# Hand-written engine orders made anew in a fused attention and state-space kernel

## The chip, the cores and the metric

The kernel runs on one core of a Trainium2 chip. The core has TensorE (PE in the profile, its weight loads PEld), VectorE (DVE), ScalarE (ACT), GpSimd (POOL) and SyncE (SP), each with an instruction stream of its own that it works through in order, and 16 DMA engines behind several queues. The metric is the device time of one execution in microseconds (us); lower is better.

## The reference

Two independent computations on sequences of 2048 positions and 640 channels; their outputs are put side by side into a bf16 array of 1 x 2048 x 1280.

```python
# part A: attention, 32 heads of 20, each position sees itself and 7 positions 2, 4 .. 14 back
qkv    = x @ wqkv                                # 2048x640 @ 640x1920
logits = (q . k at the 8 positions) * 20**-0.5   # masked where the position is < 0
a      = (softmax(logits) weighted sum of v) @ wo
# part B: a state-space layer, 192 complex states for each channel
dt = exp(log_dt)
K[d, l] = Re( sum_n C[d,n] * exp(dt*A[d,n]*l) * dt*B[d,n] )      # 640 x 2048, from 640 x 192 parameters
y = irfft(rfft(u, 4096) * rfft(K, 4096))[:2048] + u * Dskip      # causal convolution of u with K
out = concat([a, y], axis=-1)
```

## The kernel before

Part B's kernel K is not made by 2048 exponentials for each state. A position l is split as l = x + 8b with 20 values of x and 33 of b, and exp(dt·A·l) becomes a product of two tables. The 640 channels are cut into five groups (c = 0 to 4) of 128. For each group, `Xtab` (20 complex rows of 192 states) and `Ytab` (33 rows) are built on DVE from a few starting powers; then `kgen_part` on TensorE multiplies them, channel by channel. These are the stages that the orders below name:

- **Prologue.** `prep` brings in the parameters and transposes them on TensorE; ACT and DVE make phases and magnitudes. `am0`, `gens0`, `genm0` make the starting powers of group 0 (ACT exponentials, ACT sines, DVE products), `am1`, `gens1`, `genm1` those of groups 1 to 4, which SP stores to DRAM (`Gdram`). `weights` forms C·dt·B on DVE and has SP store it. `load` brings in the transposes of x (20 in all, 5 for each quarter of the sequence) and constants.
- **Projections** `k0 q0 v0 … v3`: three for each quarter of the sequence, each 25 matmuls of 128 x 512 (L515), five ACT copies (L516) into the tile `st`, of which there are two, and one SP store (L519 for v) to DRAM (`qkd`, `vd`).
- **Tables** of group c: `tab` (SP loads `Xg` from `Gdram`, one tile) and `taby` (five SP loads into `Ytab`, one tile, L330), `mag` (16 ACT exponentials, L345), `xtab` (32 DVE instructions, L306 and L307; `Xtab` has two tiles), `ypos` (12 on DVE, two on POOL), `yneg` (four on DVE, L351 two of them). `yneg` takes mag's two halves.
- **Table products** `kgen{c}0` to `kgen{c}3`: one opening product of zeros and 128 small ones (L398, L403) for each, then one ACT copy (L405) into `Kd`, of which there are two; PSUM tag "b", four buffers.
- **Convolution.** `u` turns u around through DRAM (`Udram`) on POOL and DVE. For each group: `u{c}` (SP loads `U`, 16 matmuls, 8 ACT copies), `spread{c}` (36 matmuls and 16, 12 copies), `spec`/`spec{c}` (128 matmuls L452, 16 copies L456: the spectra of u of group 0, and of K of group c with u of the next), `swap{c}` (SP), `prod{c}` (four DVE products), `inv{c}` (64 matmuls L479, 8 copies into Z; Z of groups 0 to 2 goes to DRAM). The last step, `last00` to `last07` and `last10` to `last13`, turns blocks of positions back with the table `HB` (four POOL loads, `hb`), adds u·Dskip (`uD`; `ud`, `ud0` to `ud4`) and stores.
- **Attention** for each quarter b: `fetch{b}` and `fetchv{b}` (SP loads `qk` and `vb` from DRAM), `logits{b}` (ten DVE products L562, 44 matmuls L566, three ACT functions, one DVE product into `attn`), `av{b}` (ten DVE products L592, 160 matmuls L598, six copies into `oT`), `out{b}` (40 matmuls L611, eight copies, four stores L614). The products of L562 and L592 share three buffers; L566's sums and L598's sums have two PSUM buffers each.

The tables' memory is released after `kgen4`; `HB`, `uD` and the Z of groups 3 and 4 lie in it. The projections' memory is released after the last projection and holds `U`, the constant `T` (cT, `load2`) and others after that.

What sets the order is the dictionary `SEQ`: for each engine a list of words, written out by hand. A word `kgen00:129` means the next 129 instructions that stage kgen00 has on this engine; a word without a number means one. The function `chain` walks the list and ties each instruction to the one before it. So each engine issues exactly in this order, SP's list being the order in which SP issues its DMAs; semaphores add what one engine waits for from another. With `at(name)` the code says which stage the instructions inside it belong to. The instructions of `magnitudes`, `gens` and the first `ymag` also go through `pin`, which ties ACT's functions to one another in the order in which the code makes them.

Of the kernel before, what the change touches and what calls it, by code (L numbers as in the profile page):

```python
# [13 lines left out]
bf16 = mybir.dt.bfloat16  # L14
# [113 lines left out]
def att_consts_np():  # L128
# [11 lines left out]
prep:30 weights:15 k0:2 weights:15 k0:2 weights:15 k0:5 weights:15 k0:16 q0:25 v0:25 k1:25 q1:25 v1:25 k2:25 q2:16 kgen00:129 q2:9 kgen01 kgen02  # L140
kgen03:129 kgen02:128 kgen01:128 v2:25 k3:10 logits0:4 k3:2 logits0:4 k3:6 logits0:4 k3:7 q3:10 logits0:8 q3:15 logits0:4 v3:10 kgen10:33 kgen11:33
kgen12 kgen13:129 logits0:4 kgen10:64 logits0:8 v3:4 logits0:4 v3:6 kgen10:32 v3:5 logits0:4 kgen11:96 kgen12:96 av0:32 kgen12:32 av0:48 u0:8 av0:5
u0:2 av0:8 u0:2 av0:9 u0:2 av0:9 u0:2 av0:17 spec:20 av0 spec:12 av0:31 spec:32 out0:4 spec out0:3 spec:31 logits1:4 out0:2 spec out0 spec:16 out0:2
spec:15 out0:3 logits1:2 u1:8 logits1:2 out0:2 u1:2 out0:2 u1:2 out0 u1:2 logits1:4 u1:2 out0:2 spread0:8 out0:2 spread0:8 logits1:2 spread0:20
logits1:2 out0 logits1:4 spread0:8 logits1:4 out0:2 spread0:4 out0:2 spread0:2 out0 spread0:2 logits1:4 spec0:32 logits1:4 spec0 out0:4 spec0:16
out0:3 spec0:16 out0:2 spec0:15 out0 spec0:48 inv0:57 kgen20:129 inv0:7 logits1:8 kgen21 kgen22 kgen23:33 u2:2 logits1:2 kgen23:32 u2:2 logits1:2
kgen23:64 u2:2 kgen22:32 u2:2 kgen22:32 u2:4 kgen22:64 u2:4 kgen21:128 spread1:36 av1:6 spread1:8 av1:5 spread1:2 av1:8 spread1:2 av1:9 spread1:2
av1:9 spread1:2 av1:27 spec1:49 av1:15 spec1:16 av1 spec1:63 inv1:64 kgen30 kgen31:33 kgen30:32 kgen31:96 kgen30:96 kgen32 kgen33 u3:2 kgen33:32 u3:2
kgen33:32 u3:2 kgen33:32 u3:4 kgen33:32 kgen32:32 u3:6 kgen32:32 spread2:16 kgen32:32 spread2:20 kgen32:32 av1:21 spread2:8 av1:5 spread2:2 av1:8
spread2:4 av1:2 spread2:2 av1:12 spec2:6 logits2:4 spec2:26 av1:8 spec2 av1:19 spec2:16 av1:5 logits2:4 spec2:31 out1:2 logits2:4 spec2 out1:2  # L150
spec2:16 out1 spec2:15 out1:2 spec2 out1:3 spec2:15 out1:20 inv2:32 out1:7 inv2:25 kgen40:33 inv2:5 logits2:4 inv2:2 out1:2 kgen40:96 logits2:4 out1
logits2:4 kgen41 kgen42 kgen43 u4:2 kgen43:64 u4:2 kgen43:32 u4:2 kgen43:32 logits2:6 u4:2 logits2:2 u4:2 logits2:4 kgen42:32 u4:4 logits2:4 kgen42:32
u4:2 spread3:8 logits2:2 kgen42:32 spread3:8 logits2:2 spread3:12 kgen42:32 spread3:8 kgen41:32 spread3:6 kgen41:32 spread3:2 kgen41:32 spread3:6
av2:15 spread3:2 av2:33 kgen41:32 spec3:32 av2:8 spec3 av2:8 spec3:95 av2:43 inv3:32 av2:21 inv3:25 spread4:16 inv3:4 spread4:12 inv3 spread4:8 inv3:2
av2:16 spread4:16 av2:16 spec4:32 logits3:4 out2:2 spec4 logits3:2 spec4:16 logits3:2 out2:2 spec4:16 logits3:4 spec4:15 out2 spec4 logits3:4 spec4:16
out2:2 spec4:15 logits3:4 spec4 out2:2 spec4:15 logits3:4 out2:20 inv4:32 out2 logits3:4 out2:5 inv4:25 last00:18 inv4:7 logits3:12 out2:5 last01
logits3:2 last01:8 logits3:2 last01 last02 last01:8 last02:17 last03 av3:32 last03:9 last04 last03:8 av3:17 last04:17 av3:37 last05 av3:39 last05:17
av3:35 last06:10 out3:10 last06:8 out3:10 last07 out3:10 last07:17 last10:34 last11:17 out3:10 last11:17 last12:34 last13:34
""",
    mybir.EngineType.Activation: """  # L160
prep:11 am0:2 prep am0:9 weights:2 gens0:13 weights gens0:4 weights gens0:4 k0 gens0 mag0:3 k0 mag0:3 k0 mag0:2 k0 mag0:3 k0 mag0:2 q0 mag0:3 am1:11
gens1:5 q0:3 gens1 q0 v0:3 gens1 v0:2 gens1:2 k1:2 gens1 k1 gens1 k1 gens1 k1 gens1 q1 gens1 q1 gens1 q1 gens1 q1 gens1 q1 v1 gens1:2 v1 gens1 v1
gens1 v1:2 k2:2 gens1:2 k2:2 mag1:5 k2 mag1:3 q2:2 mag1:8 q2 kgen00 q2:2 kgen03 kgen02 kgen01 v2:5 k3:5 q3:5 mag2:16 kgen13 v3:2 logits0:2 v3:2 kgen10
v3 logits0:2 kgen11 kgen12 av0:2 u0:8 av0:2 spec:4 av0:2 spec:4 out0 spec:4 out0 spec:4 out0 u1:7 spread0:4 u1 out0 spread0:8 out0:2 spec0:6 out0
spec0:10 mag3:14 inv0:4 mag3:2 inv0:3 out0 kgen20 inv0 logits1:2 u2:2 logits1:2 kgen23 u2:4 kgen22 u2:2 kgen21 spread1:12 av1:2 spec1:16 mag4:8 inv1:7
mag4 inv1 mag4:7 kgen31 kgen30 u3:5 kgen33 u3:3 spread2:4 kgen32 spread2:8 av1:2 spec2:6 av1 spec2:4 av1 spec2:4 out1 spec2:2 out1:5 inv2:4 out1
inv2:4 kgen40 out1 u4:3 kgen43 u4:4 logits2:2 u4 spread3:2 logits2 spread3 logits2 spread3 kgen42 spread3:8 kgen41 spec3:16 av2:2 inv3:4 av2:2 inv3:3
spread4:4 inv3 spread4:8 av2:2 spec4:10 out2 spec4:6 out2:3 inv4:2 out2 inv4:2 out2:2 inv4:3 last00:2 inv4 logits3:2 out2 last01 logits3:2 last01
last02:2 av3:2 last03:2 av3:2 last04:2 av3:2 out3 last05:2 out3:3 last06:2 last07:2 out3:4 last10:2 last11:2 last12:2 last13:2
""",  # L170
    mybir.EngineType.DVE: """
prep:11 gens0 prep gens0:2 prep:2 gens0:2 genm0 gens0:2 genm0 gens0:2 genm0 gens0:2 genm0 gens0:2 genm0 gens0:2 genm0 gens0:2 genm0 gens0:2 genm0
gens0:2 genm0 gens0 weights genm0 ypos0 genm0 weights:10 xtab0 weights xtab0 gens1 xtab0:2 gens1 xtab0:2 gens1 xtab0:2 gens1 xtab0:2 u xtab0:8 gens1
genm1 xtab0 genm1 xtab0 gens1 xtab0:2 genm1 xtab0:4 gens1 xtab0:4 gens1 xtab0:2 gens1 ypos0 genm1 gens1:2 ypos0 gens1 genm1 gens1 ypos0 gens1 genm1
gens1 ypos0 gens1 genm1 gens1 ypos0 genm1 gens1:2 ypos0 gens1 genm1 gens1 ypos0 genm1 yneg0 gens1 yneg0 ypos0:2 genm1 ypos0:2 u yneg0:2 xtab1:22 u
xtab1:4 logits0 xtab1:4 logits0 xtab1:2 logits0 ypos1:2 logits0 ypos1:2 logits0 ypos1:2 logits0 ypos1:4 yneg1 ypos1:2 yneg1:2 u xtab2:2 yneg1 xtab2:2
logits0 xtab2:2 logits0 xtab2:2 logits0 xtab2:2 logits0 xtab2:8 logits0 xtab2 av0:8 xtab2 av0:2 xtab2 ypos2 xtab2 logits1 xtab2:4 logits1 xtab2:4
logits1 xtab2:2 logits1 ypos2 logits1 ypos2:2 logits1 ypos2:2 logits1 ypos2:2 logits1 ypos2 xtab3 ypos2 yneg2 ypos2:2 yneg2 xtab3 yneg2 prod0 xtab3
prod0:2 xtab3 prod0 xtab3:2 yneg2 xtab3:2 logits1 xtab3:2 logits1 xtab3:10 logits1 xtab3:2 av1 xtab3:4 av1 xtab3:4 av1 xtab3:2 ypos3:4 av1 ypos3:2
xtab4 ypos3:2 av1 ypos3:2 yneg3 ypos3:2 yneg3 xtab4 prod1 xtab4 prod1:2 xtab4 prod1 xtab4:2 yneg3 xtab4:2 yneg3 xtab4:2 av1 xtab4:2 av1 xtab4:2 av1  # L180
xtab4:18 av1:2 ypos4:2 logits2 ypos4:4 logits2 ypos4:2 logits2 yneg4 ypos4 yneg4 ypos4 prod2 ypos4 prod2:2 ypos4 prod2 yneg4 logits2 yneg4 logits2:7
av2:7 prod3:3 av2 prod3 av2 ud1 ud4 ud0 ud2 ud3 av2 logits3:6 prod4:3 logits3 prod4 logits3:4 av3:10
""",
    mybir.EngineType.Pool: """
load ypos0 load:6 prep:18 load:7 ypos0 u:13 load2:4 u ypos1:2 kgen03:4 u:6 logits0:7 ypos2:2 kgen13:4 ypos3:2 kgen23:4 ypos4:2 kgen33:4 hb kgen43:4
hb:3
""",
    mybir.EngineType.SP: """
prep:12 load:15 weights k0 weights genm1:2 q0 genm1 v0 genm1:2 k1 genm1:3 q1 genm1:2 v1 genm1 k2 tab1 fetchv0:8 fetch0:2 q2 fetch0 taby1:5 v2 tab2
fetch0:2 k3 fetch1 q3 fetch1:2 v3 u0 load2 taby2:2 fetchv1:4 taby2:3 u1 fetchv1:4 out0 fetch1 swap0:2 tab3 u2 fetch1 out0 fetch2:2 out0:2 fetch2 swap1  # L190
inv0 swap1 u3 taby3:3 tab4 taby3:2 fetchv2:4 swap2:2 inv1 u4 taby4:5 fetchv2:4 fetch2 out1:3 fetch2 swap3:2 inv2 fetch3 out1 fetch3:2 last00:3
last01:3 fetchv3:4 ud swap4:2 fetchv3:4 fetch3:2 out2:3 last02:3 last00:4 out2 last03:3 last04:3 last01 last02:4 last01 last05:3 last06:3 last01:2
last03:4 last07:3 last04:4 last05:4 out3:2 last06:4 last07:2 out3 last07:2 out3 last10:4 last11:4 last12:4 last13:4
""",
}

def partB_prep(tc, pools, early, Gd):

    nc = tc.nc
    V = nc.vector
    pp, psp, ident = pools["prep"], pools["psum"], pools["ident"]
    Wd = NCH * CW
    nat, ldt = early
    hp = pp.tile([128, 1], f32, name="half_pi")
    nc.gpsimd.memset(hp[:], float(np.pi / 2))
    pools["half_pi"] = hp[:]
    dtb = pp.tile([128, NCH], bf16, name="dtb")
# [408 lines left out]
def kernel(  # L618
# [17 lines left out]
    nc = tc.nc  # L636
# [311 lines left out]
```

## Time and profile before

| | |
|---|---|
| runs, each the time of one execution | 412.6, 424.4, 828.71 us; median 424.4 |
| span of the profiled execution | 415.1 us |
| granted TensorE clock in it, mean | 0.889 of full speed |
| busy: PE, PEld, DVE, ACT, POOL | 316.8, 196.1, 307.1, 262.1, 50.4 us |
| DMA moved | 70.67 MB in 78841 packets, of them 35264 under 512 B |

The profiled execution's own time is its span, 415.1 us; it lies between the two lower runs. A stretch of the timeline shows, in this order: from and to, length, then for PE, PEld, DVE, ACT and POOL the busy time and the number of instructions, the granted clock, the busy share of the DMA engines, and GB/s. In a timeline each row is: when the instruction began, how long it took, its engine, its line, its operation, and its tiles; in brackets the idle time of that engine just before it and what ended that idle time ("issue": nothing that the profile shows). A row may stand for several alike (x13). In SyncE's queue (SPq) the rows are DMA issues.

### The profile page before, as it was taken

Reading aid. Unit: us, or ns where it says so; the run is one execution under the profiler, and the core shown is the slowest. Engines: PE = TensorE matmul, PEld = TensorE weight load, DVE = VectorE, ACT = ScalarE, POOL = GpSimd, SP = SyncE. Lnnn points to the kernel's source line nnn. Section 1 sums busy time; section 2 is a strip of 40 time slices with the busy share of each in tenths; the row PEclk is TensorE's granted clock in tenths of the full one; section 3 lists DMA queues with packets and bytes.
Section 4 is the critical chain, followed back from the end, with each engine's and each line's share of the span. In section 5 each row is a group of like instructions: output and inputs, shape, how many; then the busy total and the mean of one; then the engine's idle time right before and its main releaser. Section 6 shows DMA issues by size and latency. Waiting matters only on the chain. (4 is left out here: it accounts for less than half of the span.)

```text
span 415.1 us, 13105 instructions
## 1 busy us (share of the span) xinstructions
PE 316.8 (76%) x5645; PEld 196.1 (47%) x5654; DVE 307.1 (74%) x445; ACT 262.1 (63%) x570; POOL 50.4 (12%) x101
## 2 busy tenths in 40 slices
PE   0569249989359988799788886799999875897781
PEld 0224114335233355356476556565666663475561
DVE  0558978995974999589999599959972765786500
ACT  0587977987004533489976596469747977573552
POOL 7453300004014010200000200011000400000000
PEclk9999959999759999589979696779999988799996
DMA  5999765668998847869308530727166499616656
GB/s 75 217 212 178 202 164 190 214 216 260 207 213 205 271 126 171 233 146 254 114 17 230 154 86 2 205 64 154 51 195 209 138 369 313 137 49 177 160 134 95
DMA packets 78841, 70.67 MB, mean 170 GB/s; under 512 B 35264, under 2 KB 73904, under 8 KB 76992
## 3 DMA queue, kind: packets, MB, share of 16 engines
q1 hardware_dynamic: 71616, 54.96, 51.3%
q0 software_dynamic: 4144, 12.18, 11.9%
q10 hardware_dynamic: 3024, 2.70, 2.9%
q8 instruction: 44, 0.72, 0.7%
q14 instruction: 13, 0.11, 0.1%
HBM read 37.82 MB, written 23.65 MB: 148 GB/s over the span
## 5 line engine op out<-in xcount | busy, mean ns | idle before, releaser
L515 PE MATMUL ps_p<-xT,w 128*128 128x512 bf16 x291 | 76.4, 409 | 20.9 <-ACT st L516 15.4
L515 PEld LDWEIGHTS <-w 128*128 128x128 bf16 x300 | 30.0, 103 | 60.3 <-issue 33.3
L562 DVE TENSOR_TENSOR prod<-qk 128x2048 bf16<-128x2048 bf16 x40 | 48.2, 1225 | 11.6 <-PE ps_l L566 8.9
L592 DVE TENSOR_TENSOR p<-vb,attn 128x2048 bf16<-128x2048 bf16 x40 | 47.4, 1224 | 12.1 <-PE ps_o L598 12.0
L438 ACT CAST A<-ps_f 128x512 bf16<-128x512 f32 x80 | 42.8, 613 | 19.0 <-PE ps_f L437 18.6
L516 ACT CAST st<-ps_p 128x512 bf16<-128x512 f32 x60 | 34.6, 586 | 23.1 <-PE ps_p L515 21.1
L456 ACT CAST Sp<-ps_f 128x512 bf16<-128x512 f32 (+1 forms) x96 | 42.4, 564 | 4.6 <-PE ps_f L452 3.5
L398 PE MATMUL ps_k<-Ytab,Xtab 128*20 128x33 bf16 x1280 | 29.7, 248 | 15.1 <-issue 15.1
L598 PE MATMUL ps_o<-p,cHs 64*32 64x256 bf16 x640 | 27.7, 297 | 12.5 <-DVE p L592 7.7
L452 PE MATMUL ps_f<-A,cT 64*128 64x128 bf16 (+1 forms) x768 | 29.4, 211 | 5.4 <-ACT Sp L456 3.5
L398 PEld LDWEIGHTS <-Xtab 128*20 128x20 bf16 x1280 | 23.3, 128 | 21.6 <-issue 20.2
L405 ACT CAST Kd<-ps_k 128x264 bf16<-128x264 f32 x20 | 7.6, 380 | 40.7 <-PE ps_k L403 40.5
L479 PE MATMUL ps_ia<-cE,Sp 128*128 128x128 bf16 x160 | 25.5, 254 | 8.0 <-DVE Sp L467 7.8
L452 PEld LDWEIGHTS <-cT 64*128 64x128 bf16 x768 | 21.7, 96 | 18.4 <-issue 17.1
L403 PE MATMUL ps_k<-Ytab,Xtab 64*20 64x33 bf16 x1280 | 27.4, 244 | 3.5 <-issue 3.5
L611 PE MATMUL ps_op<-wo,oT 128*128 128x320 bf16 x160 | 29.0, 301 | 0.7 <-ACT ob L612 0.6
L480 ACT CAST Z<-ps_ia 128x512 bf16<-128x512 f32 x40 | 22.4, 604 | 10.7 <-PE ps_ia L479 8.3
L403 PEld LDWEIGHTS <-Xtab 64*20 64x20 bf16 x1280 | 22.4, 123 | 8.0 <-issue 6.7
L479 PE MATMUL ps_ia<-cE,UT 128*128 128x128 bf16 x160 | 25.4, 253 | 0.0
L306 DVE TENSOR_TENSOR Xtab<-Xtab,Xg 128x768 bf16<-128x768 bf16 (+2 forms) x35 | 24.5, 699 | 0.3
L307 DVE TENSOR_TENSOR krtmp<-Xtab,Xg 128x768 bf16<-128x768 bf16 (+2 forms) x35 | 24.4, 698 | 0.0
L345 ACT ACTIVATE mag<-ta 128x192 bf16<-128x192 f32 x80 | 22.6, 397 | 1.2 <-DVE Ytab L351 1.2
(109 smaller groups left out, 571.0 us busy)
## 6 DMA issues: line engine op xcount, KB each, us to landing
qk<-qkd SPq DMA_DIRECT2D x20, 263.0 KB, 5.3
qkd<-st SPq DMA_DIRECT2D x8, 640.0 KB, 5.3
UT<-Sp SPq DMA_DIRECT2D x10, 512.0 KB, 6.7
Gdram<-cs SPq DMA_DIRECT2D x11, 384.0 KB, 3.0
HB<-k_HB POOLq DMA_DIRECT2D x4, 1024.0 KB, 16.1
vb<-vd SPq DMA_DIRECT2D x16, 196.5 KB, 5.0
Xg<-Gdram SPq DMA_DIRECT2D x4, 768.0 KB, 7.7
Zdram<-Z SPq DMA_DIRECT2D x3, 1024.0 KB, 8.6
```

The lines of the kernel that those rows point to most:

```text
L398: MM(o, lhsT=X[:, :, part, col], rhs=Y[:, :, part, col], start=False, stop=False, tile_position=(0, 32 * g), skip_group_check=True)
L403: MM(o, lhsT=X[hb:hb + 64, :, part - 2, col], rhs=Y[hb:hb + 64, :, part - 2, col], start=False, stop=(part == 3), tile_position=(hb, 32 * ...
L438: nc.scalar.copy(out=A1[:].rearrange("p k r s t -> p (k r) s t")[:, :, sig, 8 * q:8 * q + 8], in_=ps[:])
L452: nc.tensor.matmul(ps[h][:, kk], lhsT=C["T"][hs, k, 64 * (1 - r):64 * (1 - r) + 128], rhs=A1[hs, k, r, s0:s1, :].rearrange("p s t -> p (s ...
L456: nc.scalar.copy(out=o, in_=ps[h][:].rearrange("p k (s t) -> p s t k", t=64))
L479: nc.tensor.matmul(ps[:, i], lhsT=X[:, h, 4 * t:4 * t + 4, :].rearrange("p g k -> p (g k)"), rhs=C["E"][:, n_, :], start=(i == 0 and n_ == ...
L515: nc.tensor.matmul(ps[:], lhsT=self.w[which][:, kt, 128 * ct:128 * ct + 128], rhs=self.xT[:, kt, 512 * sc:512 * sc + 512], start=(kt == 0) ...
L516: nc.scalar.copy(out=st[:, ct], in_=ps[:])
L562: V.tensor_tensor(out=pr[:], in0=self.qk[b][ct][:, 0, HALO:].unsqueeze(1).to_broadcast([128, 4, PB]), in1=windows(self.qk[b][ct][:, 1, 8 - ...
L592: V.tensor_tensor(out=p2[:], in0=windows(self.v[b][t][:, 2 * qp:2 * qp + 2, 0:PH], 2, 4), in1=at[:].unsqueeze(2).to_broadcast([128, 4, 2, ...
L598: nc.tensor.matmul(ps[half][32 * q:32 * q + 32, t % 2], lhsT=C["Hs"][r], rhs=p2[r, m, q2, :], start=(t % 2 == 0 and m == 0), stop=(m == 3) ...
L611: nc.tensor.matmul(ps[:], lhsT=oT[:, t, 128 * s:128 * s + 128], rhs=self.wo_sb[:, t, 320 * eh:320 * eh + 320], start=(t == 0), stop=(t == 4))
```

## The change

Every list of `SEQ` is written anew, with all the instructions of the old ones. Around it, five edits of the code:

```diff
@@ partB_prep
-    hp = pp.tile([128, 1], f32, name="half_pi")
-    nc.gpsimd.memset(hp[:], float(np.pi / 2))
-    pools["half_pi"] = hp[:]
@@ PartA.load_w
-        self.nc.scalar.dma_start(out=t[:], in_=self.wqkv.rearrange("(kt k) c -> k kt c", k=128)[:, :, D * i:D * i + D])
+        self.nc.sync.dma_start(out=t[:], in_=self.wqkv.rearrange("(kt k) c -> k kt c", k=128)[:, :, D * i:D * i + D])
@@ the order of the activation tables
-    tail = []
     def pin(ins):
-        if tail:
-            tc.add_manual_dep(ins.ins, tail[-1], mybir.DependencyInfo(mybir.DependencyClass.NoSync, mybir.DependencyReason.DATA), reason="order of the activation tables")
-        tail.append(ins.ins.name)
         return ins
@@ the prologue
-    with at("prep"):
+    with at("set"):
+        hp = pp.tile([128, 1], f32, name="half_pi")
+        nc.gpsimd.memset(hp[:], float(np.pi / 2))
+        pools["half_pi"] = hp[:]
+        zw = cst.tile([128, 128], bf16, name="zw")
+        nc.gpsimd.memset(zw[:], 0.0)
+        pools["zero"] = zw[:]
+    with at("params"):
...
-        for i in range(5):
-            a.load_x(i)
-        for nm in "kqv":
-            a.load_w(nm)
+    with at("params2"):
         for i, nm in enumerate(("B_C_re", "B_C_im", "B_B_re", "B_B_im")):
             par(nm, nat[2 + i], [nc.gpsimd])
-        zw = cst.tile([128, 128], bf16, name="zw")
-        nc.gpsimd.memset(zw[:], 0.0)
-        pools["zero"] = zw[:]
+    for nm in "kqv":
+        with at("w" + nm):
+            a.load_w(nm)
+    for sc in range(4):
+        with at(f"x{sc}"):
+            for i in range(5):
+                a.load_x(5 * sc + i)
+    with at("prep"):
         ta, wi, weights = partB_prep(tc, pools, (nat, ldt), Gd)
     with at("load"):
-        for i in range(5, 20):
-            a.load_x(i)
```

So half_pi and the zeros come first on POOL; the three weight loads go to SP; the twenty transposes and the weights are stages that SP's list can place singly. `pin` ties nothing any more; ACT's list still fixes ACT's order.

The lists, SP's in full up to the fourth group, the others where the work around the first two groups' products and the end lies:

```diff
 SP
-prep:12 load:15 weights k0 weights genm1:2 q0 genm1 v0 genm1:2 k1 genm1:3 q1 genm1:2 v1 genm1 k2 tab1 fetchv0:8 fetch0:2 q2 fetch0 taby1:5 v2 tab2
-fetch0:2 k3 fetch1 q3 fetch1:2 v3 u0 load2 taby2:2 fetchv1:4 taby2:3 u1 fetchv1:4 out0 fetch1 swap0:2 tab3 u2 fetch1 out0 fetch2:2 out0:2 fetch2 swap1
-inv0 swap1 u3 taby3:3 tab4 taby3:2
...
+params:7 wk x0:5 wq x1:4 x3 wv x1 k0 x2:5 x3 weights q0 x3 genm1:2 v0 genm1:2 k1 weights genm1 q1 genm1:6 k2 fetch0:2 tab1 q2 fetch0 taby1:5 fetchv0
+x3:2 fetchv0:2 v1 tab2 v2 fetch0 fetchv0 fetch0 fetch1 k3 taby2 q3 fetchv0:3 v3 taby2 u0 load2 fetchv0 taby2:2 u1 swap0 tab3 fetch1:2 swap0 taby2
+fetchv1:3 out0 taby3 fetch1:2 u2 taby3 fetchv1 taby3:2 fetchv1 out0 fetch2 out0 fetch2 taby3 inv0 swap1 tab4 swap1 u3 taby4:2
...
 PE
...
-k2:25 q2:16 kgen00:129 q2:9 kgen01 kgen02
-kgen03:129 kgen02:128 kgen01:128 v2:25 k3:10 logits0:4 k3:2 logits0:4 k3:6 logits0:4 k3:7 q3:10 logits0:8 q3:15 logits0:4 v3:10 kgen10:33 kgen11:33
-kgen12 kgen13:129 logits0:4 kgen10:64 logits0:8 v3:4 logits0:4 v3:6 kgen10:32 v3:5 logits0:4 kgen11:96 kgen12:96 av0:32 kgen12:32 av0:48 u0:8
...
-last03 av3:32 last03:9 last04 last03:8 av3:17 last04:17 av3:37 last05 av3:39 last05:17
-av3:35 last06:10 out3:10 last06:8 out3:10 last07 out3:10 last07:17 last10:34 last11:17 out3:10 last11:17 last12:34 last13:34
...
+k2:25 q2:9 kgen00 kgen01:29 kgen02:21 kgen00:12 q2:7 kgen00:3
+kgen01:12 kgen00:3 kgen03:3 kgen02:15 kgen03:10 kgen00:11 q2:4 kgen01:2 q2:3 kgen00:2 kgen03 kgen01:2 kgen03 kgen02:6 kgen03:5 kgen00 kgen03:6 kgen01
+kgen00:5 kgen02:7 v2 q2:2 kgen02 v2:2 kgen00:2 v2 kgen00 kgen01:4 kgen03:24 v2:4 kgen03:4 kgen00:12 kgen02:11 kgen00 logits0 kgen00:5 kgen01:9
+logits0:10 kgen03:18 kgen00:15 kgen01:20 v2:5 kgen00:2 kgen03:7 kgen02:30 v2:10 kgen00:2 kgen03:9 kgen01:2 kgen00:3 logits0 v2:2 kgen01:29
...
+k3 kgen01:5 kgen00:13 k3
+kgen03:12 kgen01:4 kgen00 kgen02:6 kgen00:4 kgen02:6 k3:23 logits0:12 q3:25 v3:17 logits0:10 kgen10:8 kgen11:3 kgen12:3 kgen11:3 v3:8 kgen12:22
...
+kgen13:16 u0:16 av0:21 spec:128 u1:16 av0:13 spread0:16
...
+inv0:58 kgen20:129 kgen21:17 kgen22:9
...
+spec2:26 av1:32
+out1:8 logits2:4 out1:7 inv2:64 kgen40:111 kgen41:8 kgen40:18
...
+kgen43:19 u4:2 kgen43:98
...
+last04:4 last05:18 av3:37 last06:18 av3:54 last07:18 av3:37 last10:34 last11:11 av3:32 last11:14 last12 last11:9 out3:11 last12:33 last13:11 out3:9
+last13:23 out3:20
 ACT
-prep:11 am0:2 prep am0:9 weights:2 gens0:13
...
-mag1:8 q2 kgen00 q2:2 kgen03 kgen02 kgen01 v2:5 k3:5 q3:5 mag2:16 kgen13
...
+params:6 prep:2 mag0:15 am0:8 gens0:9 weights:3
...
+k2:5 gens1 mag1:12 q2:5 v2:5 k3:3 kgen02 kgen01 mag2:2 k3 mag1:3 kgen03
+k3 mag2:2 q3:3 mag1 q3 kgen00 q3 v3:5 mag2:12 logits0:4 kgen11 kgen12 kgen10 u0:8 kgen13 spec:16 u1:8 spread0:4 av0:2
...
 DVE
...
-ypos0:2 genm1 ypos0:2 u yneg0:2 xtab1:22 u
-xtab1:4 logits0 xtab1:4 logits0 xtab1:2 logits0 ypos1:2 logits0
...
-yneg1
...
-xtab2:8 logits0 xtab2 av0:8 xtab2 av0:2 xtab2 ypos2
...
-ud3 av2 logits3:6 prod4:3 logits3 prod4 logits3:4 av3:10
...
+ypos0:3 yneg0:2 u logits0:3 xtab1:32 logits0 ypos1:8 yneg1:2 logits0:2 ypos1:3 logits0:2
+xtab2 ypos1 yneg1:2 logits0 xtab2:9 logits0 xtab2:19 logits0 av0:4 xtab2:3 ypos2:12 av0:6 xtab3:3 logits1:2 yneg2:2 logits1 yneg2:2 prod0:4 logits1:3
+xtab3:24 logits1:4 xtab3:5 ypos3:10 yneg3:2 ypos3:2 yneg3:2 logits1 xtab4:6 prod1:4 av1:3 xtab4:26 ypos4:7 av1 ypos4:5 av1:6 logits2 yneg4 logits2
+prod2:4 yneg4:3 logits2:9 av2:3 ud1 ud2 prod3:4 ud0 av2:7 logits3:4 ud3 prod4:4 ud4 logits3:7 av3:10
 POOL
-load ypos0 load:6 prep:18 load:7 ypos0 u:13 load2:4 u
...
+set u params2:2 load:2 ypos0 params2:11 u params2:3 set ypos0 u:18 load:6 ypos1:2 kgen03 load2:2
...
```

POOL's old list has all fourteen instructions of `load` ahead of `u`; the new one has two ahead of it and twelve behind. Kgen's four parts, formerly mostly one after another, now go in turns with each other and with the projections and logits around them.

## The prediction

> **What bounds the kernel now.** I read the page's first block, then the busy time by stretches, the total of waits, and the order in time of VectorE (DVE), TensorE's weight loads (PEld) and SyncE's DMA queue (SPq).
>
> ```profile
> PE 316.8 (76%) x5645; PEld 196.1 (47%) x5654; DVE 307.1 (74%) x445; ACT 262.1 (63%) x570; POOL 50.4 (12%) x101
> ...
> 0.00:97.30 97.30, 61.89 (x276) 26.72 (x281) 72.73 (x142) 70.82 (x140) 25.82 (x49) 0.93 0.83 185
> 97.30:146.20 48.90, 35.96 (x633) 18.98 (x635) 34.90 (x56) 16.04 (x39) 10.61 (x19) 0.83 0.94 237
> 146.20:211.90 65.70, 55.50 (x1144) 34.60 (x1146) 58.96 (x81) 44.86 (x110) 4.31 (x14) 0.86 0.60 160
> 211.90:278.70 66.80, 54.54 (x1500) 41.66 (x1499) 57.85 (x92) 43.73 (x96) 2.65 (x7) 0.81 0.42 116
> 278.70:345.80 67.10, 60.75 (x1320) 41.60 (x1314) 46.70 (x46) 51.40 (x106) 7.06 (x14) 0.97 0.64 194
> 345.80:415.10 69.30, 48.18 (x787) 32.55 (x785) 35.93 (x31) 35.30 (x85) 0.00 (x0) 0.90 0.60 140
> ```
>
> No engine is full. DVE works 307.1 of 415.1 us and idles 24.6, 14.0, 6.7, 9.0, 20.4 and 33.4 us in the six stretches (length less the fifth number). An order that kept DVE fed would pay; one that blocks an in-order queue loses. Three places matter.
>
> ```profile
> 97.25 0.56 DVE L353 TENSOR_SCALAR Ytab<-Ytab 128x1536 bf16<-128x1536 bf16 x1
> 102.34 0.36 DVE L306 TENSOR_TENSOR Xtab<-Xg 128x384 bf16<-128x384 bf16 x1 [4.53 <-DMA Xg<-Gdram]
> ...
> 131.85 1.23 DVE L562 TENSOR_TENSOR prod<-qk 128x2048 bf16<-128x2048 bf16 x1 [6.03 <-PE ps_l L566]
> ```
> ```profile
> 113.54 0.27 PEld L398 LDWEIGHTS <-Xtab 128*20 128x20 bf16 x13 [6.20 <-issue]
> ...
> 120.56 0.27 PEld L398 LDWEIGHTS <-Xtab 128*20 128x20 bf16 x13 [4.56 <-issue]
> ...
> 131.19 0.12 PEld L566 LDWEIGHTS <-cGs 128*32 128x32 bf16 x4 [0.42 <-issue]
> ```
> ```profile
> 122.29 2.52 SPq L330 DMA_DIRECT2D Ytab<-Gdram  x5
> 129.75 0.37 SPq L519 DMA_DIRECT2D vd<-st  x1
> ...
> 159.25 0.36 SPq L519 DMA_DIRECT2D vd<-st  x1
> 159.78 0.39 SPq L820 DMA_DIRECT2D U<-Udram  x1
> 160.22 1.02 SPq L669 DMA_DIRECT2D cT<-k_T  x1
> 168.38 0.80 SPq L330 DMA_DIRECT2D Ytab<-Gdram  x2
> ```
>
> Call **G** the moment table products may start: the second L351 of yneg0 ends, 97.3 in the profile. DVE then waits 4.53 us for Xg and later 6.03 us for TensorE, which stood still 6.20 and 4.56 us inside kgen0 with nothing to wait for that the profile shows. The queue rows matter most: the U and cT loads go out at 159.8, ahead of taby2 (168.4), because the old list has them before it; they need only v3 done. kgen1's last product ends at 168.2, and taby2 cannot go earlier, since its tile Ytab has one buffer.
>
> **The change, part by part.** All counts below are of the new list; the instructions themselves are the old ones.
>
> *Prologue.* ACT loses three weight issues (4.42 to 10.33), half_pi is set first on POOL (its old place held a sine 1.12 us, at 24.80). Against that, 15 of mag0's exponentials go ahead of am0 at a pitch of 0.26 (nine took 2.38 us): 4 us. First sine about 19 instead of 23.3; am1 begins near 35 instead of 43.7, since it must wait for genm0. DVE's weights need B_im, whose 16 POOL loads keep nearly their places, so DVE reaches xtab0 near 41 (41.2 before). From there to G lie the same 51 us of DVE work and formerly 4 us of idle. G comes at 94: **-3 us**. Bounds: -8 (sines and B_im both 5 earlier), +3 (the w loads, now on SP among the transposes, hold q0 or v0).
>
> *DVE after G.* neg and u 1.2, three logits products 3 x 1.15, xtab1 15.4 (its pieces from 102.34 to 123.89 without what lies between): ends G+20.3, and the Xg wait is covered. A gain of 4.5 at this place.
>
> *TensorE after G.* 512 products and 4 openers of kgen0 at 0.0213 (2.72 us for a part without stall) 11.0; 43 projection matmuls (q2 16, v2 25, k3 2) at 0.243, 10.4; twelve visits to projections at 0.33 extra (0.12 of idle into kgen, 0.21 out) 4.0; three to logits 1.7. kgen0 ends at **G+28** (old: G+24.7, but with v2 still to do, 6.5). The stalls of 6.20 and 4.56 I count as gone. The change between kgen parts in mid-run costs nothing to 0.12 each (old rows kgen30/kgen31: 0.0; 60 of them here, 181 instead of 19 in all): 0 to 7 us here, 0 to 19 in all; taken as 0, the nearest rows.
> The Trainium skill, "TensorEngine Tiling (Array Packing)", Tiling Modes, says that changing the tiling mode drains TensorE, which speaks against table products between projections. The row that looks like such a drain is the 0.42 of idle at each change between projections and logits; kgen and projections show 0.11 and 0.12. At 0.42 each way the twelve visits would cost 10 us instead of 4, and kgen0 would end at G+34.
>
> *First block on SP.* The new list reads `taby1:5 fetchv0 x3:2 fetchv0:2 v1 tab2 v2`. taby1 waits for kgen0's last product, and behind it now stand the last two transposes of x3 (k3's matmuls wait), v1's store (k3's first ACT copy waits for its buffer `st`) and v2's store. Issues: 5 x 0.5, 0.6, 2 x 1.36, 1.3: v1's store at G+35.2, landed 5.5 later, G+40.7. A transpose issued at G+31 lands 6.6 later, so k3 starts in earnest near G+38, ends at G+45 behind the copies, then logits, q3 (25 x 0.243), v3:17: **kgen1 starts G+58** (146.2 = G+48.9 before). ACT is in order: mag1's last exponentials stand behind k3 and q3, so yneg1's second half waits until G+50. DVE idles from G+21.5 to G+31 for Ytab and some 5 more.
>
> *Second block.* kgen1 11, v3:8 2, logits and changes 4: ends G+75. The list `taby2 q3 fetchv0:3 v3 taby2 u0 load2` puts U and cT behind that end plus 4 us of issues: G+79. cT needs 11.6: spec starts **G+91** (178.9 = G+81.6 before), 16 copies at 0.34, u1 8 at 0.51. av0's fifth DVE product stands behind u0, spec and u1 on TensorE, by the buffer it reuses: G+100. DVE has run out at G+90: 10 us idle, 3 more by G+110. spread0, spec0 and prod0 follow; kgen2 starts G+127 (G+117.4).
>
> *Third.* kgen2 in 15 us, G+142. u2's load stands behind taby3, which waits for kgen2: 2 + 3.9, then 8 copies at 0.51, spread1 12 at 0.52, spec1 16 at 0.50: prod1 at G+167 (250.19 = G+152.9). u2 was long done before. inv1, kgen3 until G+194 (G+181).
>
> *Later.* ypos4, seven av1 products and two logits on DVE (20 us) and about 6 of waiting for Ytab lie between kgen3's end and prod2: G+220 (293.9 = G+196.6). logits2 are spread through kgen4 and spread3, attn some 11 later still; av2 and uD, on which DVE lost 5.9 and 4.4, run closer, and prod4 comes at G+291.5 (364.0 = G+266.7). Seven logits left, not four: av3's last product ends at 415.5, not 389.8: **+25.7**, the G gain included.
>
> *Tail.* After it 91 matmuls of the last blocks instead of 172 (0.05 each), the same 40 of out3 (0.13), 21 SP issues instead of 39 (0.46): TensorE saves 4, the queue 8: **-8**, since the chain of waits ends on that queue.
>
> **The sum.** 415.1 + 25.7 - 8 = 432.8, against the profiled execution. Runs were 412.6, 424.4 and 828.7; the median is 9.3 above the span, the middle of the first two, 418.5, is 3.4 above. I predict **436**.
>
> **Rivals.**
>
> *DVE is fed (faster, 394).* If the blocks are shorter than DVE's stock of work, they cost nothing. For it: 15.4 us of xtab1 and 15 of xtab2 stand ready beside the blocks; 97 fewer changes between unlike stages at about 0.25 is 24 us of TensorE. Against it: products wait on buffers in order. It would take 9 of the 14.0 idle of the second stretch (4.53 and 6.03 mostly), 8 in the tail, 4 in the prologue: 415 - 21 = 394. It decides when kgen0 ends by G+20 and U and cT go out by G+68. Chance 0.22.
>
> *Losses and gains cancel (415).* The blocks at half (13), less 3 more in the prologue and 8 to 10 in the tail: 412 to 420. Chance 0.16.
>
> *Short runs slow TensorE too (450).* 181 kgen changes at 0.12 break the fourfold overlap of column groups, and stalls of 3 to 6 us return in kgen20:129, kgen40:111 and kgen43:98. 12 to 18 on top. The row against it is 0.0 at kgen30/kgen31. Chance 0.12. This is also how the change would not do what it says: between projections, yet no denser.
>
> **How the numbers follow.** The forecast has 0.50, its own range 424 to 446. Two per cent is about what a measurement of this kernel tells from no change. Faster 0.22, within 0.16, slower 0.62 (0.50 and 0.12). For 8 in 10 the range reaches half into the faster rival and the slow one: **402 to 456**.
>
> **What would show it.** Right: in SyncE's queue the last two transposes and a vd store just after five Ytab loads; ACT's copy of k3 held by the DMA vd<-st; U and cT issued after kgen1's last product; a DVE gap near 10 us before the fifth av0 product, released by PE ps_o; U again behind Ytab for u2; under 20 us after the last L592. Each step wrong: G outside 89 to 100; kgen0 over G+34 or under G+24, or still with stalls of over 3 us; kgen1 before G+52; spec before G+84. If DVE's idle in the third stretch stays under 8 us, the forecast is wrong and the first rival holds.

## The result, and the profile after

The changed kernel takes 450.2 us (median; 450.0 to 453.1). The ratio to the kernel before is 1.088, 95% interval 1.077 to 1.099. Some executions of before were slower than its others, and the ratio is taken against the undisturbed ones, near 414 us. The forecast had slower, and three of the places where the time went, but 436: the sum said +17.7 on the profiled span, and the spans show +33.3 (415.1 to 448.4). Where the missing 15.6 us arose is the main subject below.

The page's first block of the changed kernel, and behind it its busy time by stretches (columns as for the kernel before), cut at the moments that the prediction names: G, kgen1's start, kgen2's start, prod1, kgen3's end, prod2, prod4, the end of av3's last product.

```profile
PE 321.2 (72%) x5641; PEld 203.4 (45%) x5654; DVE 315.9 (70%) x445; ACT 259.3 (58%) x570; POOL 50.1 (11%) x101
```
```profile
0.00:93.00 93.00, 61.57 (x269) 26.48 (x274) 76.31 (x143) 70.02 (x138) 24.60 (x45) 0.89 0.97 213
93.00:148.70 55.70, 43.55 (x652) 21.66 (x659) 41.92 (x68) 17.30 (x39) 6.52 (x12) 0.88 0.57 151
148.70:216.90 68.20, 47.05 (x1130) 33.99 (x1130) 49.86 (x64) 40.69 (x98) 8.58 (x23) 0.82 0.52 133
216.90:265.20 48.30, 31.30 (x769) 21.76 (x766) 36.45 (x59) 28.06 (x67) 3.22 (x7) 0.86 0.48 132
265.20:298.70 33.50, 28.98 (x689) 21.82 (x695) 21.89 (x33) 19.37 (x47) 0.00 (x0) 0.75 0.01 3
298.70:329.70 31.00, 11.83 (x269) 7.88 (x257) 19.94 (x22) 10.65 (x23) 2.70 (x6) 0.67 0.65 155
329.70:396.10 66.40, 56.90 (x1280) 41.45 (x1280) 43.79 (x40) 46.56 (x105) 4.45 (x8) 0.87 0.72 220
396.10:431.70 35.60, 28.36 (x420) 19.86 (x419) 25.76 (x22) 18.45 (x42) 0.00 (x0) 0.87 0.63 154
431.70:448.40 16.70, 11.68 (x191) 8.53 (x189) 0.00 (x0) 8.23 (x18) 0.00 (x0) 0.91 0.63 123
```

No engine got more work that explains this. VectorE's sum is 8.8 us higher with the same 445 instructions, but the kernel of the experiments with everything mended has 315.7 us and takes 406. The granted clock was 0.846 in the mean instead of 0.889, and TensorE's busy time grew by 4.4 us only. What grew is idle time. In the sixth row TensorE works 11.83 of 31.00 us. In the fifth it is busy (28.98 of 33.50 us), but the DMA engines move 3 GB/s: SyncE issues nothing from 257.3 to 299.1, since the head of its list waits for the last table product of group 3. Set beside the prediction's own sums (differences of the moments in it):

| stretch | before | forecast | measured | off by |
|---|---|---|---|---|
| start to G | 97.3 | 94.0 | 93.0 | -1.0 |
| G to kgen1's start | 48.9 | 58.0 | 55.7 | -2.3 |
| to kgen2's start | 68.5 | 69.0 | 68.2 | -0.8 |
| to prod1 | 35.5 | 40.0 | 48.3 | **+8.3** |
| to kgen3's end | 28.2 | 27.0 | 33.5 | **+6.5** |
| to prod2 | 15.5 | 26.0 | 31.0 | **+5.0** |
| to prod4 | 70.1 | 71.5 | 66.4 | -5.1 |
| to av3's last product | 25.8 | 30.0 | 35.6 | **+5.6** |
| to the end | 25.3 | 17.3 | 16.7 | -0.6 |

SyncE's queue in order of time (a row: start, length, queue, line, DMA, tiles):

```profile
120.05 2.24 SPq L327 DMA_DIRECT2D Ytab<-Gdram  x5
...
122.80 2.46 SPq L492 DMA_TRANSPOSE xT<-in_A_x_dram  x2
...
126.42 0.45 SPq L516 DMA_DIRECT2D vd<-st  x1
...
164.80 0.35 SPq L327 DMA_DIRECT2D Ytab<-Gdram  x1
...
169.72 0.95 SPq L819 DMA_DIRECT2D U<-Udram  x1
170.72 0.92 SPq L661 DMA_DIRECT2D cT<-k_T  x1
...
231.57 0.34 SPq L327 DMA_DIRECT2D Ytab<-Gdram  x1
...
232.94 0.47 SPq L819 DMA_DIRECT2D U<-Udram  x1
...
235.90 0.41 SPq L611 DMA_DIRECT2D out_dram<-ob  x1
...
299.10 0.80 SPq L327 DMA_DIRECT2D Ytab<-Gdram  x2
...
302.68 2.88 SPq L327 DMA_DIRECT2D Ytab<-Gdram  x2
```

Three times a Ytab load waits for table products (to 120.05, 164.80, 231.57), and what others need stands behind it: transposes and v1's store, U and cT, U and a store of out0. Who waited for them, first in ScalarE's timeline, then in that of TensorE's weight loads; the last fence has one row of TensorE's products:

```profile
132.29 1.07 ACT L513 CAST st<-ps_p 128x512 bf16<-128x512 f32 x2 [15.53 <-DMA vd<-st]
...
242.66 0.43 ACT L609 CAST ob<-ps_op 128x320 bf16<-128x320 f32 x1 [10.74 <-DMA out_dram<-ob]
```
```profile
101.92 0.64 PEld L395 LDWEIGHTS <-Xtab 128*20 128x20 bf16 x37 [0.42 <-issue]
102.66 0.33 PEld L512 LDWEIGHTS <-w 128*128 128x128 bf16 x3
103.41 0.12 PEld L395 LDWEIGHTS <-Xtab 128*20 128x20 bf16 x1 [0.42 <-issue]
...
180.27 2.14 PEld L434 LDWEIGHTS <-U 128*128 128x128 bf16 x11 [15.72 <-DMA U<-Udram]
...
239.42 0.83 PEld L434 LDWEIGHTS <-U 128*128 128x128 bf16 x5 [7.88 <-DMA U<-Udram]
...
285.29 0.95 PEld L400 LDWEIGHTS <-Xtab 64*20 64x20 bf16 x48
...
292.75 0.12 PEld L400 LDWEIGHTS <-Xtab 64*20 64x20 bf16 x3 [0.41 <-issue]
...
298.67 0.15 PEld L400 LDWEIGHTS <-Xtab 64*20 64x20 bf16 x2
298.73 0.15 PEld L595 LDWEIGHTS <-cHs 64*32 64x32 bf16 x2
312.82 0.56 PEld L595 LDWEIGHTS <-cHs 64*32 64x32 bf16 x15 [13.94 <-issue]
```
```profile
312.82 1.04 PE L595 MATMUL ps_o<-p,cHs 64*32 64x256 bf16 x16 [13.69 <-DVE p L589]
```

The first ScalarE row, the two U rows and SyncE's rows up to 232.94 are as forecast. The rest is not: out0's copy held for 10.74 us; table products of group 3 (L400), of which the bulk ended at 286.24, still going at 298.67; and then 13.69 us in which TensorE waits for a product of VectorE. VectorE's rows show first its gap in front of av0's fifth product, which was forecast, then what the late table products held back:

```profile
184.66 1.23 DVE L589 TENSOR_TENSOR p<-vb,attn 128x2048 bf16<-128x2048 bf16 x1 [16.22 <-PE ps_o L595]
...
301.66 0.36 DVE L303 TENSOR_TENSOR Ytab<-Ytab 128x384 bf16<-128x384 bf16 x1 [14.19 <-DMA Ytab<-Gdram]
...
309.71 0.76 DVE L303 TENSOR_TENSOR Ytab<-Ytab 128x1152 bf16<-128x1152 bf16 x1 [6.96 <-DMA Ytab<-Gdram]
```

Waits for Ytab cost it 14.19 and then, inside ypos4, 6.96 us more, because taby4's third and fourth load went out (302.68) behind other DMAs.

### The profile page after: what moved, and what is told of

Read it like the earlier page. It is cut to its first block, busy times and chain, and to the rows that moved or that the text cites. A ratio compares the mean times of both kernels' runs of the same rounds, so it can differ in the third digit from the quotient of the medians.

```text
span 448.4 us, 13103 instructions
## 1 busy us (share of the span) xinstructions
PE 321.2 (72%) x5641; PEld 203.4 (45%) x5654; DVE 315.9 (70%) x445; ACT 259.3 (58%) x570; POOL 50.1 (11%) x101
## 3 DMA queue, kind: packets, MB, share of 16 engines
q0 software_dynamic: 4144, 12.18, 10.5%
## 5 line engine op out<-in xcount | busy, mean ns | idle before, releaser
L512 PE MATMUL ps_p<-xT,w 128*128 128x512 bf16 x287 | 81.5, 433 | 28.6 <-ACT st L513 21.0
L512 PEld LDWEIGHTS <-w 128*128 128x128 bf16 x300 | 31.2, 108 | 72.3 <-issue 48.3
L595 PE MATMUL ps_o<-p,cHs 64*32 64x256 bf16 x640 | 24.0, 311 | 21.6 <-DVE p L589 18.0
L395 PE MATMUL ps_k<-Ytab,Xtab 128*20 128x33 bf16 x1280 | 36.3, 246 | 2.6 <-issue 2.6
L434 PE MATMUL ps_f<-cBU,U 128*128 128x256 bf16 x80 | 19.0, 385 | 26.5 <-DMA U<-Udram 22.9
L303 DVE TENSOR_TENSOR Ytab<-Ytab 128x384 bf16<-128x384 bf16 (+2 forms) x15 | 13.3, 890 | 28.5 <-DMA Ytab<-Gdram 28.2
L395 PEld LDWEIGHTS <-Xtab 128*20 128x20 bf16 x1280 | 26.6, 128 | 14.2 <-issue 10.2
L400 PE MATMUL ps_k<-Ytab,Xtab 64*20 64x33 bf16 x1280 | 29.6, 241 | 0.0
L608 PE MATMUL ps_op<-wo,oT 128*128 128x320 bf16 x160 | 25.4, 301 | 1.7 <-ACT oT L599 0.9
L434 PEld LDWEIGHTS <-U 128*128 128x128 bf16 x80 | 11.2, 156 | 32.6 <-DMA U<-Udram 23.6
L595 PEld LDWEIGHTS <-cHs 64*32 64x32 bf16 x640 | 12.8, 101 | 28.4 <-issue 21.6
L400 PEld LDWEIGHTS <-Xtab 64*20 64x20 bf16 x1280 | 22.8, 122 | 6.1 <-issue 3.2
L476 PE MATMUL ps_ia<-cE,Sp 128*128 128x128 bf16 x160 | 22.1, 235 | 4.0 <-DVE Sp L464 3.9
```

The costliest lines, as they stand in the source:

```text
L303: V.tensor_tensor(out=full(O), in0=full(Y), in1=gb(gr), op=A.mult)
L395: MM(o, lhsT=X[:, :, part, col], rhs=Y[:, :, part, col], start=False, stop=False, tile_position=(0, 32 * g), skip_group_check=True)
L400: MM(o, lhsT=X[hb:hb + 64, :, part - 2, col], rhs=Y[hb:hb + 64, :, part - 2, col], start=False, stop=(part == 3), tile_position=(hb, 32 * ...
L434: nc.tensor.matmul(ps[:, :, 4 * j:4 * j + 4], lhsT=sv[:, :, 2 * q + j], rhs=C[mat][:].rearrange("p (k g) -> p k g", g=4), start=(j == 0), ...
L512: nc.tensor.matmul(ps[:], lhsT=self.w[which][:, kt, 128 * ct:128 * ct + 128], rhs=self.xT[:, kt, 512 * sc:512 * sc + 512], start=(kt == 0) ...
L595: nc.tensor.matmul(ps[half][32 * q:32 * q + 32, t % 2], lhsT=C["Hs"][r], rhs=p2[r, m, q2, :], start=(t % 2 == 0 and m == 0), stop=(m == 3) ...
```

## The experiments

Two theories. **QUEUE**: work that is ready stands behind an instruction that waits, in SyncE's list at three places, in TensorE's list at kgen33. **SHORT RUNS**: table products in turns of a few make TensorE itself slower. **COVERED** stands for "the wait is real, but what follows would have waited anyway". The kernel before was run beside each group of experiments; its medians there lay from 416 to 422 us, so the changed kernel's 450.2 is taken as the measure for kernels made from it. The changed kernel itself was not run again beside them, so a gain of a few us rests on the stretches of the traces as well, which are given where it matters.

**All three places of SyncE's list.** Only order is edited:

```diff
-genm1:6 k2 fetch0:2 tab1 q2 fetch0 taby1:5 fetchv0 x3:2 fetchv0:2 v1 tab2 v2 fetch0
+genm1:6 v1 k2 fetch0:2 tab1 q2 fetch0 v2 taby1:5 fetchv0:3 tab2 fetch0
-k3 taby2 q3 fetchv0:3 v3 taby2 u0 load2 fetchv0 taby2:2
+k3 q3 fetchv0:3 v3 u0 load2 fetchv0 taby2:4
-out0 taby3 fetch1:2 u2 taby3 fetchv1 taby3:2 fetchv1 out0 fetch2
+out0 u2 fetch1:2 out0 taby3:2 fetchv1 taby3:2 fetchv1 fetch2
```

(x3's two transposes join the one before them.)

> The changed kernel (450.2 us), with SyncE's list alone edited: x3's last two transposes, v1's store and v2's store go out before the five taby1 loads, u0 and load2 before taby2, u2, fetch1 and out0's second store before taby3. Theory QUEUE (issues stuck behind Ytab loads that wait for table products hold TensorE and ScalarE): k3's two waits (6.17 and 3.69 us) and ScalarE's 15.53 us for the vd store vanish, TensorE's 16.72 us in front of u0 shrink below 4, ScalarE's 10.74 us in front of out0's copy vanish; VectorE's own work then binds, so not all of it is won: 420 to 432 us. Rival SHORT RUNS (kgen's products in turns of a few make TensorE slower): these waits only hide that, 443 us or more.

Measured: 423.7 us (423.1 to 427.1), ratio 1.015 [1.008, 1.022]. Its queue:

```profile
146.59 0.38 SPq L819 DMA_DIRECT2D U<-Udram  x1
...
163.37 1.75 SPq L327 DMA_DIRECT2D Ytab<-Gdram  x4
...
196.35 0.38 SPq L819 DMA_DIRECT2D U<-Udram  x1
...
217.78 0.81 SPq L327 DMA_DIRECT2D Ytab<-Gdram  x2
```

Each U load now leaves some 17 and 21 us before the Ytab loads that used to stand in front of it. 26.5 us are won by moving DMA issues alone. In this run's totals of waits ScalarE no longer waits for v1's store, its waits for stores of out0 are 0.9 us (10.7), and TensorE's for U 0.7 (22.9). QUEUE holds; SHORT RUNS, which had 443 or more, does not.

**The places one by one**, each with its lines of the diff above alone:

> The changed kernel (450.2 us) with the first place of SyncE's list alone mended: x3's two transposes, v1's store and v2's store ahead of taby1. In the run with all three places mended k3 ended 15.3 us earlier and kgen1 began 6.5 earlier, but ended only 1.4 earlier. Theory QUEUE, as the prediction has it: each place delays what follows by its own wait, 440 to 445 us. Rival COVERED: kgen1 waits for VectorE's second table anyway and the first place costs next to nothing, 446 to 451.

> The changed kernel with the second place of SyncE's list alone mended: u0 and load2 ahead of taby2's first two loads. QUEUE: TensorE's wait for U in front of u0 goes from 16.7 us to under 5, spec starts near 170 instead of 184.9; 431 to 440 us. Rival COVERED: VectorE and the later blocks take it up, 445 or more.

> The changed kernel with the third place of SyncE's list alone mended: u2, fetch1 and out0's second store ahead of taby3. QUEUE: TensorE's 7.9 us for U and ScalarE's 10.74 us for out0's store go, u2 starts near 231 instead of 239.4; 438 to 444 us, a term that the prediction put at some 6. Rival COVERED: 447 or more, and then the 10 us that the mended run gained between kgen2's start and prod1 came from elsewhere.

Measured: 444.9, 440.6 and 442.6 us, that is 5.3, 9.6 and 7.6 less than 450.2 (ratios 1.054 [1.050, 1.059], 1.040 [1.032, 1.048], 1.048 [1.044, 1.053]). The first lies at the edge of its interval, the second just above its own; no COVERED is met. In the traces kgen2 starts at 212.42 with the first place mended and at 206.37 with the second, 4.5 and 10.5 us earlier than in the changed kernel (216.89). With the second place mended, TensorE's row for U stands without a wait:

```profile
168.63 2.15 PEld L434 LDWEIGHTS <-U 128*128 128x128 bf16 x11
```

In the run of the third place, kgen2's start to prod1 took 37.7 us (220.5 to 258.2) instead of 48.3, though kgen2 started 3.6 later. Together the three give 22.5, 4 less than mended at once.

**kgen33 in one piece**, TensorE's list alone:

```diff
-kgen32:2 kgen33:17 u3:5 av1:5 u3:3 av1:17 u3:8 spread2:14 kgen33:3 spread2:34 av1:12 spread2:4 kgen33:6 av1:2 kgen33:20 av1:23
+kgen32:2 kgen33:46 u3:5 av1:5 u3:3 av1:17 u3:8 spread2:48 av1:12 spread2:4 av1:25
```

> The changed kernel with TensorE's list alone edited: kgen33's last 29 products, which stand behind u3, spread2 and av1, follow directly on its first 100. QUEUE (here TensorE's queue: those 29 hold back taby4 and with it VectorE): the first taby4 load goes out near 287 instead of 299.1, VectorE's 14.2 us of idle before ypos4 fall to about 3, 438 to 443 us. SHORT RUNS: no more than 2 us of change, 448 to 451.

Measured: 439.8 us (437.2 to 441.9), ratio 1.051 [1.044, 1.059]: 10.4 us for the place of 29 products. VectorE in this run:

```profile
289.45 0.36 DVE L302 TENSOR_TENSOR Ytab<-Ytab 128x384 bf16<-128x384 bf16 x1 [3.17 <-DMA Ytab<-Gdram]
...
296.63 0.76 DVE L302 TENSOR_TENSOR Ytab<-Ytab 128x1152 bf16<-128x1152 bf16 x1 [6.09 <-DMA Ytab<-Gdram]
```

14.19 of idle became 3.17; the second wait stayed.

**Parts in turn.** The slots of table products in TensorE's list stay where they are, filled part by part (181 changes between parts become 34):

```diff
-q2:9 kgen00 kgen01:29 kgen02:21 kgen00:12 q2:7 kgen00:3 kgen01:12 kgen00:3 kgen03:3 kgen02:15 kgen03:10 kgen00:11 q2:4
+q2:9 kgen00 kgen01:29 kgen02 kgen01:32 q2:7 kgen01:18 kgen03:39 q2:4
...
```

> The changed kernel with TensorE's list alone edited: the places of table products among the other stages stay, but within a group the products fill them part by part, so changes from one part to another fall from 181 to 34. QUEUE: nothing that waits has moved, 446 to 452 us. SHORT RUNS: the kgen stretches get 12 to 18 us shorter in all, 432 to 440.

Measured: 453.4 us (451.8 to 454.5), ratio 1.084 [1.078, 1.090]: 1.4 above QUEUE's interval, and not a microsecond is won. From first to last product of kgen2, 14.4 us pass in both kernels (216.89 to 231.31, 219.27 to 233.64). SHORT RUNS is dead on this count, as the row at kgen30/kgen31 in the profile of before had said.

**Everything mended**: the three places, kgen33, and taby4's five loads together:

```diff
-taby4:2 fetch2 out0 swap2 fetchv1:2 taby4:2 fetchv1 swap2 inv1 fetchv2:5 taby4 fetchv2:3
+taby4:5 fetch2 out0 swap2 fetchv1:3 swap2 inv1 fetchv2:8
```

> The changed kernel with all three places of SyncE's list mended, kgen33's last 29 products put directly behind its first 100, and taby4's five loads without fetches between them. QUEUE: the gains of 26.5 and 10.4 us add, and taby4 in one piece takes some 4 of the 7 us of idle inside ypos4: 408 to 414 us, below the kernel before (415 to 419). Rival COVERED: once the largest wait is gone the next one binds, 416 to 424.

> The changed kernel with all three places of SyncE's list mended and kgen33's last 29 products directly behind its first 100, but taby4's loads still with other DMAs between them. In the run that had taby4 in one piece too (406.0 us), kgen3's end to prod2 took 24.6 us, in the changed kernel 31.0. Theory QUEUE: taby4's scattered loads cost 5 to 6 us on VectorE's path, 410 to 414 us. Rival COVERED: the shorter stretch came with the products, 405 to 408 us.

Measured: 406.0 us (404.8 to 407.9), ratio 0.962 [0.957, 0.966], so faster than both kernels and 2 us below QUEUE's interval; and 411.4 us (408.4 to 416.0) with taby4 scattered, ratio 0.995 [0.989, 1.001], inside its own. VectorE's timeline, first with taby4 in one piece, then scattered:

```profile
267.31 0.25 DVE L307 TENSOR_TENSOR Ytab<-Ytab,krtmp 128x192 bf16<-128x192 bf16 x1
267.60 0.76 DVE L302 TENSOR_TENSOR Ytab<-Ytab 128x1152 bf16<-128x1152 bf16 x1
```
```profile
266.57 0.25 DVE L307 TENSOR_TENSOR Ytab<-Ytab,krtmp 128x192 bf16<-128x192 bf16 x1
272.99 0.76 DVE L302 TENSOR_TENSOR Ytab<-Ytab 128x1152 bf16<-128x1152 bf16 x1 [6.16 <-DMA Ytab<-Gdram]
```

The 6.16 us are there or not with the order of the loads; kgen3's end to prod2 takes 24.6 against 31.1 us, 6.5 less, and the time differs by 5.4. The two kernels ran beside different executions of the kernel before (422.2 and 416.3 in the median), so the wait in the trace is the firmer number.

**The tail.** In the mended kernel, all av3 products of TensorE (and ScalarE's av3 copies) go ahead of last07, last10 and the first part of last11:

```diff
-av3:37 last06:18 av3:54 last07:18 av3:37 last10:34 last11:11 av3:32 last11:14
+av3:37 last06:18 av3:123 last07:18 last10:34 last11:25
```

> The mended kernel of 406.0 us with the end of TensorE's and ScalarE's lists edited: last07, last10 and the first part of last11, 63 products, stand behind av3's last product instead of between its pieces. If the new list's shorter tail (16.9 us from av3's last product to the end, 25.3 before) comes from the work put into av3's waits, 63 products at 0.05, their copies and their 12 stores come back at the end: 410 to 415 us. If those waits were not empty, av3 ends earlier by as much: 404 to 408.

Measured: 406.4 us (402.4 to 409.5) against 406.0, in the interval of the second expectation. The stretches from prod4 to av3's last product and from there to the end:

```profile
350.30:384.10 33.80, 26.77 (x390) 18.36 (x388) 25.79 (x22) 17.43 (x39) 0.00 (x0) 0.86 0.65 158
384.10:404.40 20.30, 14.89 (x225) 10.93 (x224) 0.00 (x0) 9.11 (x20) 0.00 (x0) 0.90 0.54 104
```

In the mended kernel they are 35.2 and 16.9. Behind av3 it got 3.4 us longer, ahead of it 1.4 shorter: 54.1 against 52.1 from prod4 on, while prod4 itself came 2.1 earlier here, and the end did not move. 2 us of the 4 to 9 that the first expectation named came back at most. For these 63 products a shorter tail after av3 is mostly a longer stretch ahead of it; what the other 5 of the tail's 8.6 us are was not tested.

**Two without a verdict.** The kernel before with the new order of SyncE at two places, of which the lines follow, and the kernel before with the new prologue, whose edit is the changed kernel's code and lists up to G:

```diff
-prep:12 load:15 weights k0 ... v1 genm1 k2 ... taby1:5 v2
+prep:12 load:13 weights k0 ... genm1 k2 ... taby1:5 load:2 v1 v2
-v3 u0 load2 taby2:2
+v3 taby2:2 u0 load2
```

> The kernel before (fast runs near 414 to 417 us), with SyncE's list alone edited toward the new one: x3's last two transposes and v1's store behind taby1, and taby2's first two loads ahead of u0 and load2. QUEUE: U and cT go out near 169 instead of 159.8, k3 starts some 5 us later; 422 to 432 us. SHORT RUNS, or a kernel before that has cover for this: within 2%, 412 to 420.

Measured: 425.1 us (417.7 to 428.0) against 418.7 (415.4 to 422.2) of before. The median lies where QUEUE put it, but the runs overlap; it decides nothing.

> The kernel before with the new code and the new lists up to the moment table products start (G, 97.3 in its profile, 93 in the changed one; on SyncE v1's store and x3's last transposes early), and the old lists from there. If the prologue's gain carries to the end: 3 to 5 us below the kernel before on the same chip, ratio 0.988 to 0.993. Rival: the old lists' first blocks wait for TensorE (projections, instruction fetch) and not for G, ratio 0.997 to 1.005.

Measured: 416.2 us (404.9 to 421.1) against 416.3 (409.1 to 424.7). The spread is larger than the 4 us that were sought. Whether the prologue's gain reaches the end by itself stays open.

## Why the prediction was right in direction and short by half

**Prologue, kgen0.** G came at 93.0 (forecast 94), but not step by step: the first sine began at 16.85 (19) and xtab0 at 37.0 (41), and from there to G it took 56 us, not 53. kgen0 ended 26.8 us after G (28; the terms as written add up to 27.1). Its stalls of over 3 us are gone, as counted. The price of a visit was misread, in the forecast and in its rows of before. The 0.42 is idle time of the weight loads alone. TensorE's products have none there (nor at 131.19 in the profile of before, where the projection's products run until 131.26):

```profile
101.92 0.81 PE L395 MATMUL ps_k<-Ytab,Xtab 128*20 128x33 bf16 x37
102.66 0.82 PE L512 MATMUL ps_p<-xT,w 128*128 128x512 bf16 x3
103.42 0.24 PE L395 MATMUL ps_k<-Ytab,Xtab 128*20 128x33 bf16 x1
```

From the last load of table products before this visit (102.56) to the first behind it (103.41) pass 0.85 us, of which three projection products at 0.243 are 0.73: the visit costs 0.12 in all, not 0.33. Twelve such visits are 1.4 us, not 4.0. That kgen0 ended near its forecast is in part luck, since TensorE's products also waited 0.99 and 0.74 us for ScalarE's copies (at 95.94 and 110.73), which the sum doesn't have. The Trainium skill, "TensorEngine Tiling (Array Packing)", Tiling Modes, says that a change of tiling mode drains TensorE. If this trace has such a drain, it lies within the 0.12 us, for both changes of a visit together.

**First and second block.** Right by mechanism and nearly by size: kgen1 started 55.7 us after G (58), spec 91.9 (91), kgen2 123.9 (127). ScalarE's wait for v1's store, TensorE's for U and VectorE's idle time in the third row are those forecast, though VectorE's is longer: 18.3 us (length less its busy time) instead of 13, with 16.22 instead of some 10 in front of av0's fifth product. The experiments price the two places at 5.3 and 9.6 us at the end.

**Third block: the first step that failed** (+8.3). It followed U's load behind taby3 and gave it 5.9 us. It overlooked that out0's second store stands behind taby3 as well, and that ScalarE, in order, had an out0 copy ahead of kgen22's and u2's (`kgen23 kgen21 out0 kgen22 u2:7`). U had landed by 239.4, 1.6 later than the forecast's terms give from kgen2's start; ScalarE came free at 242.66, another 3.3. The forecast also counted only the copies of u2, spread1 and spec1, and ScalarE has 2.9 us of logits1, out0 and other work between them (250.57 to 252.33, 256.13 to 257.31). The run of the third place took 10.6 us out of this stretch, 7.6 at the end; it moved U's load and the store together, so no run tells their shares apart.

**"inv1, kgen3 until G+194": the second** (+6.5). The bulk did end then, at 286.24 (G+193). But a buffer comes free with the last product, and the list puts 29 of 516 behind u3, spread2 and av1:12, at 298.7. The forecast put nothing for them. The run with kgen33 in one piece: 10.4 us.

**"About 6 of waiting for Ytab": the third** (+5.0). After kgen3's end VectorE waited 3.0 us for taby4's first load (298.7 to 301.7) and 6.96 for the third, 10 in all; the list scatters taby4 among fetches and stores that wait. One piece: 5.4 us.

**The tail: the fourth** (+5.0 over both last stretches). -8 was forecast and -8.6 came, but the work that left the tail had gone in between av3's products, and the stretch from prod4 grew by 9.8 instead of 4.2. From prod4 to the end it was 51.1 us before and is 52.3. The run of the tail shows the exchange for 3.4 us of it.

Against these stand stretches that went better than forecast, 9.2 us in all, 5.1 of them from prod2 to prod4; no experiment looked for their cause. Of the rivals, "DVE is fed" (394) comes nearest to the kernel with everything mended, 406.0, though there kgen0 still ends at G+24.5 and not by G+20. "Short runs" had 450 and so almost the measured time, by luck: its cause was wrong.

## What to carry to other kernels

For every issue that waits on compute in an in-order queue, list all that stands behind it and ask of each, stores too, who waits for it; a store that is late holds its engine's next copy and all behind that. Follow the last instruction of a group, not its bulk: 29 of 516 products in the wrong place cost 10.4 us. And price a tail together with the stretch ahead of it, since work moved across a mark may only move the mark.

## What was not expected of the hardware

Changing between table products of different parts costs nothing that these runs show: 34 changes instead of 181 in the run with parts in turn, and no time won (453.4 against 450.2). A change between table products and projections and back costs 0.12 us in all, although TensorE's weight loads stand idle for 0.42 on the way back.

In the kernel before, TensorE idled 15.1 us in L398, in long unbroken runs of table products, with nothing to wait for that the profile shows; in the changed kernel the same products (L395) idled 2.6, and in the run with parts in turn, which keeps the visits to other work, 2.6 again. The second line of products shows 3.5, 0.0 and 0.9. It is tempting to say that such stalls belong to unbroken runs. But the run with all three places of SyncE's list mended has TensorE's list of the changed kernel unaltered, and there the two lines show 2.9 and 4.9, with one stall of 4.23 us in the middle of kgen1's short turns; the kernel with everything mended shows 3.1 and 5.7. So the order of TensorE's list alone doesn't decide it, and what these stalls are is not shown.

The line of the kernel before, of the changed kernel and of the run with parts in turn, then the stall in the run with all three places mended:

```profile
L398 PE MATMUL ps_k<-Ytab,Xtab 128*20 128x33 bf16 x1280 | 29.7, 248 | 15.1 <-issue 15.1
```
```profile
L395 PE MATMUL ps_k<-Ytab,Xtab 128*20 128x33 bf16 x1280 | 36.3, 246 | 2.6 <-issue 2.6
```
```profile
L385 PE MATMUL ps_k<-Ytab,Xtab 128*20 128x33 bf16 x1280 | 33.1, 249 | 2.6 <-issue 2.6
```
```profile
156.99 0.12 PEld L400 LDWEIGHTS <-Xtab 64*20 64x20 bf16 x1 [4.23 <-issue]
```
